# Heads in pairs, wide exponentials and a mask on GpSimd in a fused chunk-selecting attention and MLP kernel

## The chip, the cores and the metric

The kernel runs on one core of a Trainium2 chip. Its time is the device time of one launch in microseconds (us); a median over several launches is quoted with its range. A launch more than 1.5% above the fastest one of the same kernel is called slow. The profile has five rows that matter here: PE (TensorE, matrix products), PEld (its weight loads, which overlap), ACT (ScalarE), DVE (VectorE) and POOL (GpSimd). The span that a profile shows is about 2 us shorter than the device time of its launch.

A few words are used throughout. PSUM is the memory that TensorE writes its results to. Both kernels use it as eight banks, each of 512 fp32 columns on 128 partitions. A "double-bank buffer" is a tile of 1024 columns. A "buffer" comes from a pool: the program asks for the next one, and the first instruction that writes it waits until everything that used it last has finished.

## The reference, cut to what matters

```python
# q, k, v: (4, 8, 768, 64) fp32; MLP: 3072 tokens, 512 -> 2048 -> 512
k_min, k_max = min/max of k over each chunk of 32 rows        # 24 chunks per head
ub  = sum over d of max(q * k_min, q * k_max)                  # bound per query and chunk
ub  = -1e9 for chunks after the query's own
top = the 6 chunks with the largest ub, for each query
scores = q @ k.T / 8, masked to the top chunks and to j <= i
attn = softmax(scores) @ v
x = attn of all heads side by side                             # (3072, 512)
h = x @ w_in;  out = (h * clip(h + 3, 0, 6) / 6) @ w_out
```

Since max(q·a, q·b) with a ≤ b equals relu(q)·b − relu(−q)·a, the bound is one matmul of [relu(q), relu(−q)] with [k_max, −k_min]. Both kernels keep it in fp32, because it decides a ranking.

## The kernel before

It is written for one core with TensorE as the engine to fill. Attention goes head by head: `stage_A` computes the chunk selection of head n, then `stage_B` computes scores, exponentials and weighted values of head n−1. The MLP of a finished batch is cut into pieces that are dealt out between the heads of the next batch, so that TensorE has MLP work while attention waits for other engines. The order of instructions on each engine is fixed when the kernel is built: a scheduler in the build chooses it, and what it knows of the buffers enters into the choice.

```python
ps_attn = pool(bufs=4, PSUM)      # four single-bank tiles for attention
ps_mlp  = pool(bufs=4, PSUM)      # four single-bank tiles for the MLP

# stage_A, one head: k and -k side by side, fp32 transposes, max over each 32 columns
nc.vector.tensor_scalar_mul(KS[:, :, D:2 * D], KS[:, :, 0:D], -1.0)
for i in range(nb):
    nc.tensor.transpose(KT[:, i * P:(i + 1) * P], KS[:, blk, :], IDENT32[:])
nc.vector.tensor_reduce(out=KC[...], in_=KT[...], axis=X, op=max)      # k statistics
nc.scalar.copy(LHS[0:64, ...], KT[0:64, ...])
...                                                  # QPM = relu(q), relu(-q), transposed
nc.tensor.matmul(UBP[:, qb, :], lhsT=QPM[...], rhs=KC[:, :], ...)      # the bound, 6 blocks
...                                                  # top 6 -> 0/1 columns next to q in CQ

# stage_B, one head: scores up to 512 wide, causal mask as a second matmul, then exp
SPS = ps_attn.tile([P, 512])
nc.tensor.matmul(SPS[:, 0:N], lhsT=LHS[...], rhs=RHS[...], ...)
nc.tensor.matmul(SPS[:, 0:P], lhsT=IDENTB[:], rhs=TRINEG[:], ...)      # first block only
nc.scalar.activation(PTt[:, 0:N], SPS[:, 0:N], Exp, bias=NEGBIG, scale=scale)
...                                                  # PVP = PT.T @ [v, 1], one tile per block
nc.vector.reciprocal(RINV[:], PVP[:, D:D + 1])
nc.vector.tensor_scalar(Xb[:, qb, ...], PVP[:, 0:D], RINV[:, 0:1], None, op0=mult)

# one MLP hidden tile of 128 features x 384 tokens
HP = ps_mlp.tile([P, 384])
...                                                  # 4 matmuls
nc.scalar.activation(U[:], HP[:], Relu, bias=THREE)
nc.vector.scalar_tensor_tensor(out=GT[:, f, :], in0=U, scalar=6.0, in1=HP, op0=min, op1=mult)
# the second product: OP = ps_mlp.tile([P, 512]), 16 matmuls, copied out and stored
```

HP's bank is therefore held through three engines: the matmuls, then U (ScalarE reads it), then GT (VectorE reads it again).

The softmax here doesn't subtract the row's maximum and nothing guards it: scores larger than these inputs give would overflow.

## Time and profile before

| reading | before |
|---|---|
| time, median of three launches | 462.2 us (459.36 to 462.56) |
| TensorE busy | 396.5 of 459.0 us |
| share of TensorE in the chain of waits | 70% |
| first attention alone (until the first HP matmul) | 124.1 us |
| attention and MLP interleaved ("middle") | 288.0 us, 269.0 of it TensorE busy |
| MLP alone at the end ("tail") | 46.9 us |

Here are three lines of the page of the kernel before: busy time with share of the span, the granted TensorE clock in 40 slices (9 is 90% or more of full speed), and the chain of work that ended last.

```profile
PE 396.5 (86%) x3052; PEld 279.6 (61%) x3072; DVE 284.3 (62%) x1213; ACT 248.8 (54%) x537; POOL 64.1 (14%) x100
...
PEclk9999657556689999999899999998999999999999
...
PE 70%; DVE 9%; ACT 7%; DMA 7%; issue 5%; ACTq 1%; DVEq 0%
```

Next, lines from the same page's table of the costliest groups. Each gives line, engine, operation, output<-inputs, shapes and count, then busy us and the mean ns of one, then the engine's idle time before them and what ended it. They are the operations that the change replaces.

```profile
L221 ACT ACTIVATE PTt<-SPS,NEGBIG 128x512 bf16<-128x512 f32 (+3 forms) x256 | 114.9, 552 | 74.3 <-PE SPS L217 74.0
L188 PE MATMUL UBP<-KC,QPM 128*128 128x24 f32 x384 | 52.7, 279 | 21.1 <-ACT QPM L184 20.5
...
L217 PE MATMUL SPS<-TRINEG,IDENTB 128*128 128x128 bf16 x192 | 44.8, 248 | 0.0
L165 PE MATMUL KT<-IDENT_64,KS 128*128 128x128 f32 x192 | 33.0, 316 | 5.0 <-DVE KS L158 4.8
```

Matmul records overlap: the record of an HP matmul lasts 326 ns (median), while HP matmuls of one tile start 160 ns apart. So what one costs a full TensorE is the distance from one start to the next. Costs of matmuls below are such distances.

The table of stretches of the kernel before gives the three stages. Its columns are the stretch, its length, busy us and instructions of PE, PEld, DVE, ACT and POOL, then the mean granted clock, the DMA share and GB/s.

```profile
0.00:124.10 124.10, 85.03 (x549) 68.98 (x550) 70.54 (x306) 45.15 (x101) 27.73 (x56) 0.74 0.64 122
124.10:412.10 288.00, 269.02 (x2272) 187.97 (x2288) 193.92 (x866) 181.86 (x398) 36.34 (x44) 0.98 0.42 60
412.10:459.00 46.90, 42.45 (x242) 22.64 (x240) 19.86 (x43) 21.79 (x38) 0.00 (x0) 0.98 0.09 34
```

In the middle TensorE idles for only 288.0 − 269.0 = 19.0 us out of 288. VectorE and ScalarE are each busy about two thirds of the time. By every view this is a TensorE kernel: take work from TensorE and it should get faster.

### The profile page before, as it was taken

Reading aid. Unit: us, or ns where it says so; the run is one execution under the profiler, and the core shown is the slowest. Engines: PE = TensorE matmul, PEld = TensorE weight load, DVE = VectorE, ACT = ScalarE, POOL = GpSimd, SP = SyncE. Lnnn points to the kernel's source line nnn. Section 1 sums busy time; section 2 is a strip of 40 time slices with the busy share of each in tenths; the row PEclk is TensorE's granted clock in tenths of the full one; section 3 lists DMA queues with packets and bytes.
Section 4 is the critical chain, followed back from the end, with each engine's and each line's share of the span. In section 5 each row is a group of like instructions: output and inputs, shape, how many; then the busy total and the mean of one; then the engine's idle time right before and its main releaser. Section 6 shows DMA issues by size and latency. Waiting matters only on the chain.

```text
span 459.0 us, 8780 instructions
## 1 busy us (share of the span) xinstructions
PE 396.5 (86%) x3052; PEld 279.6 (61%) x3072; DVE 284.3 (62%) x1213; ACT 248.8 (54%) x537; POOL 64.1 (14%) x100
## 2 busy tenths in 40 slices
PE   2267878888889998998999999887999999999996
PEld 2255656676667666755676666555676667655552
DVE  1576675555468657865687487654786578547170
ACT  0214444434458557745686467644685577567271
POOL 8221111111101101111111111111011111000000
PEclk9999657556689999999899999998999999999999
DMA  8987854424333554355343534454435432210101
GB/s 213 240 240 152 152 87 56 53 31 52 49 44 36 94 97 53 37 91 94 40 52 50 87 67 52 52 76 93 50 36 94 81 34 19 34 47 0 70 0 69
DMA packets 107307, 34.11 MB, mean 74 GB/s; under 512 B 101120, under 2 KB 101120, under 8 KB 107264
## 3 DMA queue, kind: packets, MB, share of 16 engines
q0 software_dynamic: 50176, 6.30, 21.6%
q1 hardware_dynamic: 30272, 16.78, 13.4%
q10 hardware_dynamic: 26816, 10.49, 9.3%
q8 instruction: 24, 0.39, 0.3%
q14 instruction: 19, 0.16, 0.1%
HBM read 33.55 MB, written 6.29 MB: 87 GB/s over the span
## 4 chain that ended last, share of the span: by engine, by line
PE 70%; DVE 9%; ACT 7%; DMA 7%; issue 5%; ACTq 1%; DVEq 0%
PE OP L283 16%; PE HP L269 16%; PE SPS L214 9%; PE UBP L188 8%; PE PVP L233 7%; PE KT L165 5%; ACT PTt L221 4%; DMA KS<-in_k_dram 4%; PE CQT L199 4%; PE QT L183 3%; DMA wtmpt<-in_moe_w_in_dram 3%; PE SPS L217 2%; DVE GT L274 1%; DVE KC L166 1%; DVE UBS L191 1%
## 5 line engine op out<-in xcount | busy, mean ns | idle before, releaser
L221 ACT ACTIVATE PTt<-SPS,NEGBIG 128x512 bf16<-128x512 f32 (+3 forms) x256 | 114.9, 552 | 74.3 <-PE SPS L217 74.0
L269 PE MATMUL HP<-XT,WIN 128*128 128x384 bf16 x512 | 103.1, 328 | 6.4 <-DVE GT L274 3.9
L283 PE MATMUL OP<-WOUT,GT 128*128 128x512 bf16 x364 | 91.3, 378 | 1.9 <-DVE GT L274 1.3
L273 ACT ACTIVATE U<-HP,THREE 128x384 bf16<-128x384 f32 x128 | 70.7, 591 | 26.8 <-PE HP L269 17.6
L274 DVE SCALAR_TENSOR_TENSOR GT<-U,HP 128x384 bf16<-128x384 bf16 x128 | 67.5, 546 | 11.9 <-ACT U L273 6.8
L188 PE MATMUL UBP<-KC,QPM 128*128 128x24 f32 x384 | 52.7, 279 | 21.1 <-ACT QPM L184 20.5
L269 PEld LDWEIGHTS <-WIN 128*128 128x128 bf16 x512 | 49.4, 102 | 32.7 <-issue 11.1
L188 PEld LDWEIGHTS UBP<-KC,QPM 128*128 128x128 f32 x384 | 52.0, 208 | 28.2 <-ACT QPM L184 26.5
L154 POOL DMA_DIRECT2D CQ<-in_q_dram x32 | 29.0, 907 | 238.0 <-PE SPS L214 104.1
L283 PEld LDWEIGHTS <-GT 128*128 128x128 bf16 x384 | 35.1, 99 | 33.4 <-issue 5.9
L199 PE MATMUL CQT<-IDENTB,CQ 128*88 128x128 bf16 x192 | 36.5, 261 | 18.8 <-DVE CQ L195 18.8
L238 DVE TENSOR_SCALAR Xb<-PVP,RINV 128x64 bf16<-128x64 f32 x192 | 48.2, 279 | 2.2
L233 PE MATMUL PVP<-VB,PTt 128*128 128x65 bf16 x672 | 44.9, 205 | 4.0 <-ACT PTt L221 3.2
L237 DVE RECIPROCAL RINV<-PVP 128x1 f32<-128x1 f32 x192 | 26.9, 161 | 33.7 <-PE PVP L233 32.4
L199 PEld LDWEIGHTS <-CQ 128*88 128x88 bf16 x192 | 26.1, 141 | 34.1 <-DVE CQ L195 25.7
L233 PEld LDWEIGHTS <-PTt 128*128 128x128 bf16 x672 | 35.8, 105 | 17.8 <-issue 4.5
L166 DVE TENSOR_REDUCE KC<-KT 128x16 f32<-128x512 f32 x64 | 32.9, 549 | 19.3 <-PE QT L183 14.4
L217 PE MATMUL SPS<-TRINEG,IDENTB 128*128 128x128 bf16 x192 | 44.8, 248 | 0.0
L214 PE MATMUL SPS<-RHS,LHS_163 88*128 88x512 bf16 (+3 forms) x128 | 40.3, 353 | 0.6
L214 PE MATMUL SPS<-RHS,LHS_165 88*128 88x512 bf16 (+3 forms) x128 | 40.0, 366 | 0.5 <-ACT PTt L221 0.2
L152 POOL DMA_DIRECT2D VB<-in_v_dram x32 | 26.4, 826 | 91.8 <-DVE RINV L237 72.1
L165 PE MATMUL KT<-IDENT_64,KS 128*128 128x128 f32 x192 | 33.0, 316 | 5.0 <-DVE KS L158 4.8
(424 smaller groups left out, 397.2 us busy)
## 6 DMA issues: line engine op xcount, KB each, us to landing
KS<-in_k_dram ACTq DMA_DIRECT2D x32, 192.0 KB, 3.3
QSRC<-in_q_dram SPq DMA_DIRECT2D x32, 192.0 KB, 2.7
out_dram<-OT SPq DMA_DIRECT2D x24, 256.0 KB, 2.1
VB<-in_v_dram POOLq DMA_DIRECT2D x32, 96.0 KB, 3.3
CQ<-in_q_dram POOLq DMA_DIRECT2D x32, 96.0 KB, 3.0
wtmpt<-in_moe_w_in_dram SPq DMA_DIRECT2D x4, 512.0 KB, 7.0
wtmpt<-in_moe_w_in_dram ACTq DMA_DIRECT2D x4, 512.0 KB, 6.6
wtmpt<-in_moe_w_out_dram SPq DMA_DIRECT2D x8, 256.0 KB, 3.1
```

The lines of the kernel that those rows point to most:

```text
L165: nc.tensor.transpose(KT[:, i * P:(i + 1) * P], KS[:, blk, :], IDENT32[:])
L188: nc.tensor.matmul(UBP[:, qb, :], lhsT=QPM[:, qb * P:(qb + 1) * P], rhs=KC[:, :], start=True, stop=True)
L199: nc.tensor.transpose(CQT[:, qb * P:(qb + 1) * P], CQ[:, qb, :], IDENTB[:])
L214: nc.tensor.matmul(SPS[:, 0:N], lhsT=LHS[0:D + NCH, jb * P:(jb + 1) * P], rhs=RHS[0:D + NCH, q0:q1], start=True, stop=(not first))
L217: nc.tensor.matmul(SPS[:, 0:P], lhsT=IDENTB[:], rhs=TRINEG[:], start=False, stop=True)
L221: nc.scalar.activation(PTt[:, 0:N], SPS[:, 0:N], ACT.Exp, bias=NEGBIG[:], scale=scale)
L233: nc.tensor.matmul(PVP[:, :], lhsT=PTt[:, loc:loc + P], rhs=VB[:, jb, :], start=(jb == 0), stop=(jb == qb))
L238: nc.vector.tensor_scalar(Xb[:, qb, h * D:(h + 1) * D], PVP[:, 0:D], RINV[:, 0:1], None, op0=A.mult)
L269: nc.tensor.matmul(HP[:, :], lhsT=WIN[:, kt, f * P:(f + 1) * P], rhs=XT[:, kt, :], start=(kt == 0), stop=(kt == KT_HID - 1))
L273: nc.scalar.activation(U[:], HP[:], ACT.Relu, bias=THREE[:], scale=1.0)
L274: nc.vector.scalar_tensor_tensor(out=GT[:, f, :], in0=U[:], scalar=6.0, in1=HP[:], op0=A.min, op1=A.mult)
L283: nc.tensor.matmul(OP[:, :], lhsT=GT[:, f, t * P:(t + 1) * P], rhs=WOUT[:, f, :], start=(f == 0), stop=(f == FT - 1))
```

## The change

The intent is to take work off all three busy engines at once:

- Two heads go through `stage_A` together, so that 64-row transposes become 128-row ones; k is transposed in bf16.
- k minima and maxima are taken from a separate load of k with one chunk per partition (two reductions of 2048 elements per 128 chunks), instead of from fp32 transposes.
- The score tiles of two key blocks are packed into one tile of 896 columns, so that one exp of 896 columns replaces two or three. This needs double-bank PSUM buffers.
- HP pairs go through the same double-bank buffers, with one Relu and one product of 768 columns per pair.
- The causal mask goes from a TensorE matmul to a GpSimd select on the exp's output.
- Normalisation is one reciprocal and one product for six blocks instead of twelve operations.
- Weights are cast to bf16 by the loading DMA instead of by VectorE.

The diff, cut to its core:

```diff
-    ps_attn = pool("ps_attn", bufs=4)     # single-bank
-    ps_mlp  = pool("ps_mlp",  bufs=4)     # single-bank
+    ps_big  = pool("ps_big",  bufs=2)     # double-bank: SPS, QT and HP
+    ps_sm   = pool("ps_sm",   bufs=4)     # single-bank: all the rest
...
+        KR: 128 chunks of k, one per partition (32 rows x 64)
+        view = KR[:].rearrange("p (w d) -> p d w", d=D)
+        nc.vector.tensor_reduce(out=KM[:, 0:D], in_=view, axis=AX.X, op=A.max)
+        nc.vector.tensor_reduce(out=KM[:, D:2 * D], in_=view, axis=AX.X, op=A.min, negate=True)
...
+        QT = ps_big.tile([P, 1024], FP32, name="QT", tag="big")       # two heads of q, 5 blocks
+        QP = Relu(QT);  QN = Relu(-QT)                                # ScalarE
...
-            SPS = ps_attn.tile([P, 512]); scores; mask matmul; exp up to 512 wide
+        for ja, jb in [(0, 5), (1, 4), (2, 3)]:
+            SPS = ps_big.tile([P, 1024], FP32, name="SPS", tag="big")
...
+            nc.scalar.activation(PT[:, 0:base], SPS[:, 0:base], ACT.Exp, bias=NEGBIG[:], scale=scale)
+            nc.gpsimd.affine_select(out=dv, in_=dv, pattern=[[0, 2], [1, P]], ...)   # both diagonals
...
-                    HP = ps_mlp.tile([P, GRP]); 4 matmuls; U; GT
+                HP = ps_big.tile([P, 2, 512], FP32, name="HP", tag="big")            # two at once
+                for f in range(2):
+                    for kt in range(KT_HID):
+                        nc.tensor.matmul(HP[:, f, 0:GRP], ...)
+                nc.scalar.activation(U[:], HP[:, :, 0:GRP], ACT.Relu, bias=THREE[:], scale=1.0)
+                nc.vector.scalar_tensor_tensor(out=GT[:, f0:f0 + 2, :], in0=U[:], scalar=6.0,
+                                               in1=HP[:, :, 0:GRP], op0=A.min, op1=A.mult)
```

All eight PSUM banks are used in both kernels. What changed is their form: eight tiles in two pools became two large and four small ones, and the two large ones serve three producers.

## The prediction

> **What bounds the kernel now.** TensorE. The page shows it busy 396.5 of 459 us (86%); the chain of waits puts 70% on it; ScalarE is at 54%, VectorE at 62%. The table by stretches shows three stages:
>
> - 0-115 us: start, then attention of the first batch alone. From 46 to 115 us six heads take 11.4 us each at a granted clock of 0.57-0.64, switching between 0.50 and 1.00. That is the binary clock gate of the Trainium skill, "TensorE: Matmul & The Clock Gate", Part 1; the trace agrees.
> - 115-402 us: 24 heads with three batches' MLP, 12 us per head, clock about 0.97, TensorE about 92% busy.
> - 402-459 us: the last attention, then MLP alone: four dense bursts of about 10.2 us.
>
> **What changes, from durations in the timeline and the groups.** Start-to-start at full clock: HP matmul 160 ns, OP 215 ns, fp32 transposes 110 ns each (six in 0.66 us), UBP record 117 ns, PVP 43 ns, mask matmul (TRINEG) 56 ns, bf16 transposes about 57 ns.
>
> TensorE removed:
> - 192 mask matmuls, -11 us.
> - 384 fp32 transposes become 80 fp32 + 96 bf16 + 6: 42 to 15 us, -27 us.
> - UBP goes from 384 to 320 records, bound by weight loads, -8 us.
>
> Summed, TensorE work goes from 344 to about 300 us. MLP (165 us) and PVP (30 us) are unchanged.
>
> ScalarE: exps at 388 ns (128 wide) and 691 ns (512) give 0.79 ns per column and 0.29 us fixed; 256 exps become 96 of about 1.0 us. With paired Relus and no LHS casts, 249 to about 205 us.
>
> VectorE: loses KS/QS builds, per-block normalisation (75 us to about 23), 192 compares (45 us to 7) and weight casts (13 us); gains 12 reduces over 2048 elements. Reduces of 512 (685 ns) and 256 (413 ns) extrapolate to 2.3 us each. Their stride is 256 bytes; the Trainium skill, "SBUF — State Buffer", says each access crossing a 16-byte line pays a penalty, so perhaps 4 us; no trace shows it yet. Total 284 to about 200-220 us.
>
> GpSimd: 64 casting loads at about 0.87 us, 96 masks at about 0.4 us (from 283 ns for 128, 820 ns for 768), 16 copies: 64 to about 120 us, still not the limit.
>
> **On the critical path.** Only TensorE's saving and the start count.
> - Start: first score work at about 26 us becomes about 13.
> - Attention alone: five pairs, still mostly at half clock: about 13.2 us of TensorE work, 16.5 us per pair with gaps (before 23): about 82 us.
> - Middle: 213 us of TensorE work at 88% density (two double-bank PSUM buffers shared by scores, q transposes and MLP make it slightly looser than before): 242 us.
> - Tail: 42 us of matmul plus waits for the two HP buffers (each held about 3.4 us, so 1.7 us per HP pair against 1.28 of matmul): 48 us.
>
> Sum about 384; I say **382 us, range 350 to 415**. Faster 0.96, same 0.03, slower 0.01.
>
> **What would show it.** TensorE still leads the chain; UBP group 320 records near 40 us; mask and KT fp32 groups gone; exp group 96 of about 1.0 us; reduce 2.3 us (or about 4); attention-only stage ends near 95 us, still at clock about 0.5-0.65; tail 46-50 us.
>
> **What would make it wrong.** The half clock vanishing in the attention stage (about 350). The opposite: the two double-bank buffers, or masks queued on GpSimd behind load issues, opening TensorE gaps in the middle (density 80%: about 410). Strided reduces much slower than 4 us would delay the start and k statistics. Casting weight loads could hold up k/v loads on the same queue.

## The result, and the profile after

The median is 439.37 us (438.2 to 439.62, four runs) against 461.06 us (459.36 to 462.56, four runs) of the kernel before. The ratio is 0.951, with a 95% interval from 0.945 to 0.957. Ratios are the mean time of one kernel's fast runs over that of the other's fast runs in the same rounds, so they are not quite the ratios of the quoted medians. The change is 5% faster, where 17% was predicted, and the time lies outside the range.

The lines of the page of the kernel after that answer to those shown of before:

```profile
PE 343.7 (79%) x2598; PEld 214.9 (49%) x2614; DVE 204.1 (47%) x477; ACT 191.9 (44%) x253; POOL 117.1 (27%) x211
...
PEclk9999858999889789997999999999989999999999
...
PE 51%; DVE 18%; ACT 13%; DMA 8%; POOL 5%; issue 4%; ACTq 1%; POOLq 0%
```

Work fell on every engine that was to be relieved: TensorE by 52.8 us of busy time, VectorE by 80.2 and ScalarE by 56.9. But TensorE's share of the chain fell from 70% to 51%, while VectorE's and ScalarE's nearly doubled, although both engines are now busy less than half of the time. That pattern means waiting for one another, not a new full engine.

Four groups of the same page, the new operations:

```profile
L236 ACT ACTIVATE PT<-SPS,NEGBIG 128x896 bf16<-128x896 f32 x96 | 93.1, 1005 | 48.0 <-PE SPS L230 47.6
L285 ACT ACTIVATE U<-HP,THREE 128x768 bf16<-128x768 f32 x64 | 57.7, 901 | 84.4 <-PE HP L282 83.8
L239 POOL TENSOR_SCALAR_AFFINE_SELECT PT<-PT 128x256 bf16<-128x256 bf16 x96 | 40.3, 421 | 160.6 <-ACT PT L236 160.4
L147 DVE TENSOR_REDUCE KM<-KR 128x64 f32<-128x2048 f32 x6 | 21.8, 3632 | 2.5 <-DMA KR<-in_k_dram 2.5
```

Each agrees with what was predicted for it (about 1.0 us, none given, about 0.4 us, "perhaps 4 us"). The exp also agrees with the Trainium skill, "ScalarE: Activation LUTs", What ACT_TABLE_LOAD costs, which gives 280 ns plus 0.833 ns per column for such an instruction. By that formula an estimate for 896 columns is 1026 ns; here it took 1005 ns.

The table of stretches of the kernel after, with the same three stages (until the first HP matmul, until the last PVP matmul, the rest):

```profile
0.00:97.50 97.50, 63.06 (x518) 48.38 (x519) 69.31 (x169) 38.51 (x58) 53.29 (x92) 0.89 1.13 177
97.50:377.80 280.30, 227.55 (x1800) 139.55 (x1809) 116.75 (x287) 133.63 (x170) 63.86 (x119) 0.95 0.26 36
377.80:437.70 59.90, 53.11 (x291) 26.94 (x292) 18.07 (x22) 19.80 (x25) 0.00 (x0) 0.99 0.11 40
```

This table holds the whole result. The first stage is 26.6 us shorter and the tail, which now holds more of the MLP, is 13.0 us longer. In the middle TensorE's busy time fell by 269.0 − 227.6 = 41.5 us. The middle became only 7.7 us shorter, because TensorE's idle time rose from 19.0 to 280.3 − 227.6 = 52.8 us. The work was removed, and four fifths of the gain came back as gaps.

What the gaps waited for is in the table of waits. First the kernel before, TensorE's waits in its middle stage: who waited, for whom, then us in total, how often, the longest.

```profile
PE CQT L199 <- DVE CQ L195: 4.2, 4, 1.2
PE UBP L188 <- ACT QPM L184: 4.1, 3, 1.4
PE HP L269 <- DVE GT L274: 3.9, 5, 1.2
...
PE SPS L214 <- ACT PTt L221: 0.2, 1, 0.2
```

Then the same view of the kernel after:

```profile
PE SPS L230 <- ACT PT L236: 12.3, 13, 1.6
PE SPS L230 <- DVE GT L286: 8.7, 12, 1.1
PE PVP L248 <- POOL PT L239: 7.4, 14, 1.3
PE HP L282 <- DVE GT L286: 5.5, 8, 0.7
...
PE CQT L208 <- DVE CQ_132 L201: 3.7, 2, 2.6
...
PE QT L175 <- DVE GT L286: 2.3, 4, 0.7
PE HP L282 <- ACT PT L236: 1.0, 3, 0.7
```

Line 230 writes score tiles and line 286 is the MLP's product. A score matmul does not need any result of the MLP: where SPS waits for GT, it waits for a PSUM buffer that an HP pair held until GT had read it. Scores waiting for scores cost 0.2 us in the middle before and 12.3 us now; scores waiting for the MLP did not occur before and now take 8.7 us. All waits on the two double-bank buffers together (12.3 + 8.7 + 5.5 + 2.3 + 1.0) are 29.8 us.

How such a gap comes about can be followed in the timeline of the kernel after, across the engines. Columns are start, duration, engine, line, operation, and in brackets the engine's idle time before it with what ended that. The stretch is one head's worth, near the end of the middle.

```profile
361.80 1.46 PE L282 MATMUL HP<-XT,WIN 128*128 128x384 bf16 x8 [0.68 <-DVE GT L286]
...
363.10 0.54 PE L230 MATMUL SPS<-RHS,LHS_126 88*128 88x512 bf16 x3
363.30 0.90 ACT L285 ACTIVATE U<-HP,THREE 128x768 bf16<-128x768 f32 x1 [1.24 <-PE HP L282]
364.10 1.00 ACT L236 ACTIVATE PT<-SPS,NEGBIG 128x896 bf16<-128x896 f32 x1
364.23 0.95 DVE L286 SCALAR_TENSOR_TENSOR GT<-U,HP 128x768 bf16<-128x768 bf16 x1 [1.18 <-ACT U L285]
365.15 0.92 PE L230 MATMUL SPS<-RHS,LHS_126 88*128 88x512 bf16 x5 [1.50 <-ACT PT L236]
...
366.78 0.48 PE L282 MATMUL HP<-XT,WIN 128*128 128x384 bf16 x2 [0.66 <-ACT PT L236]
...
370.99 0.32 PE L282 MATMUL HP<-XT,WIN 128*128 128x384 bf16 x1 [0.68 <-DVE GT L286]
```

At 363.1 the first buffer holds an HP pair and the second gets the first score tile. U must read the HP pair first; the exp of the score tile comes after it on ScalarE; GT reads the HP pair meanwhile. Both buffers come free at about 365.1, and TensorE, with the next score tile due in its program order, stands still for 1.50 us. The pattern then repeats: 361.80 and 370.99 are the same point of two heads, 9.19 us apart, with 0.66 + 0.68 + 1.50 = 2.84 us of gaps between them.

A count from durations alone could have pointed to this beforehand. In this stretch a head has three HP pairs and three score tiles. An HP pair holds its buffer for at least 1.28 (eight matmuls 160 ns apart) + 0.90 (U) + 0.95 (GT) = 3.13 us. A score tile holds it for at least about 1.4 us (0.4 for its matmuls, 1.0 for the exp). Three of each are 13.6 us, 6.8 us for each of two buffers, before any hand-off between engines is counted. TensorE has 9.19 − 2.84 = 6.35 us of work there. So in such a head the buffers, not TensorE, are the tighter limit. This is an estimate from the durations shown, and it holds for such heads only: the program deals out three pieces of MLP per head, and of the 24 pieces of a batch 16 are HP pairs, so four of eight heads have three pairs, two have two and two have none.

The Trainium skill, "Perfetto Trace Analysis", Optimization Strategy, describes just this sign: a gap that keeps repeating on the engine that should be saturated can mean too little PSUM for the next tile. The trace agrees: gaps of 0.68 and 1.50 us come again 9.19 us later.

### The profile page after: what moved, and what is told of

Read it like the earlier page. It is cut to its first block, busy times and chain, and to the rows that moved or that the text cites. A ratio compares the mean times of both kernels' runs of the same rounds, so it can differ in the third digit from the quotient of the medians.

```text
span 437.7 us, 6521 instructions
## 1 busy us (share of the span) xinstructions
PE 343.7 (79%) x2598; PEld 214.9 (49%) x2614; DVE 204.1 (47%) x477; ACT 191.9 (44%) x253; POOL 117.1 (27%) x211
## 4 chain that ended last, share of the span: by engine, by line
PE 51%; DVE 18%; ACT 13%; DMA 8%; POOL 5%; issue 4%; ACTq 1%; POOLq 0%
PE OP L295 16%; PE HP L282 13%; ACT PT L236 5%; PE PVP L248 5%; ACT U L285 5%; DVE GT L286 4%; DMA VB<-in_v_dram 4%; PE SPS L230 3%; PE UBP L194 3%; DVE KM L147 3%; DVE KM L148 3%; PE CQT L208 3%; PE UBP L193 3%; DMA QS<-in_q_dram 3%; POOL PT L239 2%
## 5 line engine op out<-in xcount | busy, mean ns | idle before, releaser
L236 ACT ACTIVATE PT<-SPS,NEGBIG 128x896 bf16<-128x896 f32 x96 | 93.1, 1005 | 48.0 <-PE SPS L230 47.6
L285 ACT ACTIVATE U<-HP,THREE 128x768 bf16<-128x768 f32 x64 | 57.7, 901 | 84.4 <-PE HP L282 83.8
L286 DVE SCALAR_TENSOR_TENSOR GT<-U,HP 128x768 bf16<-128x768 bf16 x64 | 61.0, 952 | 48.5 <-ACT U L285 48.4
L239 POOL TENSOR_SCALAR_AFFINE_SELECT PT<-PT 128x256 bf16<-128x256 bf16 x96 | 40.3, 421 | 160.6 <-ACT PT L236 160.4
L248 PE MATMUL PVP<-VB,PT 128*128 128x65 bf16 x672 | 40.7, 206 | 16.9 <-POOL PT L239 16.1
L248 PEld LDWEIGHTS <-PT 128*128 128x128 bf16 x672 | 32.5, 105 | 42.1 <-POOL PT L239 36.2
L193 PE MATMUL UBP<-KCBP,QP 128*128 128x48 f32 x160 | 34.2, 298 | 6.3 <-ACT QP L178 4.6
L194 PE MATMUL UBP<-KCBN,QN 128*128 128x48 f32 x160 | 34.1, 298 | 0.9 <-ACT QN L180 0.5
L193 PEld LDWEIGHTS UBP<-KCBP,QP 128*128 128x128 f32 x160 | 27.0, 212 | 9.5 <-ACT QP L178 7.5
L85 POOL DMA_DIRECT2D VB<-in_v_dram x32 | 26.6, 837 | 10.8 <-PE PVP L248 9.6
L194 PEld LDWEIGHTS UBP<-KCBN,QN 128*128 128x128 f32 x160 | 27.1, 213 | 2.4 <-ACT QN L180 2.1
L147 DVE TENSOR_REDUCE KM<-KR 128x64 f32<-128x2048 f32 x6 | 21.8, 3632 | 2.5 <-DMA KR<-in_k_dram 2.5
```

The source lines that it names most:

```text
L147: nc.vector.tensor_reduce(out=KM[:, 0:D], in_=view, axis=AX.X, op=A.max)
L193: nc.tensor.matmul(o, lhsT=QP[:, i * P:(i + 1) * P], rhs=KCBP[:, kc], start=True, stop=False)
L194: nc.tensor.matmul(o, lhsT=QN[:, i * P:(i + 1) * P], rhs=KCBN[:, kc], start=False, stop=True)
L236: nc.scalar.activation(PT[:, 0:base], SPS[:, 0:base], ACT.Exp, bias=NEGBIG[:], scale=scale)
L239: nc.gpsimd.affine_select(out=dv, in_=dv, pattern=[[0, 2], [1, P]], compare_op=A.is_ge, fill=0.0, base=0, channel_multiplier=-1)
L248: nc.tensor.matmul(PVP[:, qb, :], lhsT=PT[:, loc:loc + P], rhs=VB[:, e, j, :], start=(j == 0), stop=(j == qb))
```

## The experiments

These are the theories, with the letters that the expectations use. Theory A: the two double-bank buffers, shared by scores, q transposes and HP pairs, opened the gaps. A2, a variant: the fused pair as such (768-wide Relu and product) is too long, whatever buffer it is in. Theory B: GpSimd is the cause, by its masks and by what its queue waits for. Theory C: the slow strided k reductions on VectorE delay everything that needs VectorE. Theory D came later: weight loads crowd the first stage. All variants are edits of the kernel after and gave correct results unless said otherwise. In this summary "ratio" is to the kernel before in the same rounds.

| variant | median us (range) | ratio | first / middle / tail us |
|---|---|---|---|
| before | 461.06 (459.36 to 462.56) | 1 | 124.1 / 288.0 / 46.9 |
| after | 439.37 (438.2 to 439.62) | 0.951 | 97.5 / 280.3 / 59.9 |
| e1_hp_single | 391.84 (389.74 to 393.97) | 0.848 | 101.3 / 234.0 / 56.6 |
| e2_mask_pe | 439.96 (436.56 to 444.81) | 0.950 | 99.7 / 280.8 / 60.2 |
| e3_kstat_free (wrong) | 435.89 (433.56 to 438.76) | 0.944 | 98.0 / 273.6 / 59.9 |
| e4_vb_const | 432.12 (430.45 to 433.62) | 0.934 | 92.4 / 279.3 / 59.8 |
| e5_big3 | 432.13 (424.92 to 432.23) | none | 113.4 / 259.8 / 56.9 (slow) |
| e6_hp_single_in_big | 451.59 (450.57 to 455.84) | 0.979 | 98.6 / 295.2 / 60.3 |
| e7_unpacked | 400.01 (397.07 to 403.93) | 0.864 | 99.6 / 246.7 / 55.7 (slow) |
| e8_hp_defer | 390.49 (389.69 to 391.24) | 0.845 | 95.9 / 235.1 / 56.6 |
| e9_hp_vb_defer | 384.56 (380.21 to 388.17) | 0.834 | 88.9 / 236.0 / 56.6 |
| e10_all | 380.1 (377.89 to 381.76) | 0.826 | 92.7 / 228.0 / 56.6 |
| e11_hp_mask_pe | 394.79 (394.31 to 395.98) | 0.858 | 101.8 / 233.8 / 57.0 |
| e12_hp_kfree (wrong) | 394.81 (393.67 to 397.09) | 0.858 | 98.5 / 236.5 / 56.6 |
| e13_two_small | 469.69 (464.04 to 472.03) | 1.010 | 113.5 / 296.2 / 60.3 (slow) |
| e18_three_again (e5_big3 again) | 434.79 (431.75 to 436.28) | 0.942 | 112.0 / 263.8 / 56.9 |
| e14_three_order_of_two | 443.12 (440.81 to 446.39) | 0.961 | 110.0 / 271.5 / 57.2 |
| e17_two_order_of_three | 469.76 (464.49 to 472.78) | 1.015 | 114.7 / 285.4 / 62.7 |
| e16_after_order_of_three | 460.39 (457.85 to 463.07) | 0.998 | 111.4 / 282.1 / 62.3 |

"(slow)" marks a profile that fell on a run called slow; such a profile is not compared with others here. One caution holds for the whole table: every edit makes the build choose a somewhat different order on every engine, so a variant shows its edit together with the order that goes with it. How much an order can be worth is measured further down (e14, e16, e17).

### HP out of the double-bank buffers (e1_hp_single)

```diff
-                HP = ps_big.tile([P, 2, 512], FP32, name="HP", tag="big")     # pair, U and GT 768 wide
+                for f in range(f0, f0 + 2):
+                    HP = ps_sm.tile([P, GRP], FP32, name="HP", tag="ps")      # single, U and GT 384 wide
```

> The changed kernel with one thing undone: the MLP's first product (HP) goes one 384-wide tile at a time into the four single-bank PSUM buffers, so the two double-bank buffers serve only scores and q transposes; U and GT become 128 instructions of 384 again. Theory A (TensorE waits in the middle stage because scores, q transposes and HP share two double-bank buffers; 29.8 us of its 51 us of waits there name them): TensorE waits of scores on GT and of HP on GT go, the middle stage (289 us, from the first HP to the last attention) falls by 20 to 30 us, total 410 to 420. Theories B (masks on GpSimd) and C (k reductions on VectorE): within 4 us of 439, or some us slower for the 64 more ScalarE and VectorE instructions.

It took 391.84 us, 47.5 less than the kernel after, which is more than expected. The table of stretches of e1_hp_single:

```profile
0.00:101.30 101.30, 62.58 (x534) 48.30 (x535) 70.55 (x170) 38.59 (x58) 53.76 (x93) 0.88 1.10 170
101.30:335.30 234.00, 214.13 (x1786) 134.21 (x1794) 120.70 (x334) 142.05 (x218) 63.16 (x119) 0.99 0.31 43
335.30:391.90 56.60, 52.09 (x292) 27.18 (x291) 20.26 (x38) 23.57 (x41) 0.00 (x0) 1.00 0.11 42
```

The gain is in the middle: 46.3 of the 47.5 us. ScalarE and VectorE have more work there than in the kernel after (142.1 against 133.6 us, 120.7 against 116.8), because the narrow operations pay their fixed part twice, and yet the stage is a sixth shorter. The largest of TensorE's waits in the middle of e1_hp_single:

```profile
PE SPS L230 <- ACT PT L236: 8.3, 10, 1.1
PE CQT L208 <- DVE CQ L201: 2.5, 3, 1.3
PE QT L175 <- ACT PT L236: 2.3, 1, 2.3
PE PVP L248 <- POOL PT L239: 2.0, 8, 0.4
```

SPS no longer waits for GT at all. Of the 46.3 us, TensorE's idle time gives 52.8 − (234.0 − 214.1) = 32.9 us. The other 13.4 us are TensorE's busy time, 227.6 against 214.1 us for the same matmuls. The granted clock fits that: 0.95 in the middle of the kernel after is, with a clock of either half or full speed, some 28 us at half speed (0.05 × 280 × 2), and 0.99 is some 5 us; read in steps of 3 us, it is 27 and 7 us. Half of the difference is lost, 10 to 12 us. This is an estimate. That the gaps cause the half clock is not shown. They vanish together here, but from 358 to 376 us, where the gaps of the timeline above lie, the clock stayed full, and e18_three_again below has 20 us fewer gaps than e17_two_order_of_three at a clock of 0.91 against 0.92. The Trainium skill, "TensorE: Matmul & The Clock Gate", A second HAM failure mode: psum-queue depth-cycling, describes a case of this kind: short idling between groups of matmuls, as PSUM buffers cycle, makes the clock swing between half and full.

The waits on the mask (7.4 to 2.0 us) and on VectorE's selection (7.3 to 2.5 us, both CQT lines of after together) fell as well, though nothing was done to masks or selection. So most of these waits, too, went when the sharing ended.

### The mask back on TensorE (e2_mask_pe)

```diff
-            nc.gpsimd.affine_select(out=dv, in_=dv, ...)
+                    if c == 0:
+                        nc.tensor.matmul(SPS[:, base:base + P], lhsT=IDENTB[:], rhs=TRINEG[:],
+                                         start=False, stop=True)
```

> The changed kernel with the causal mask back on TensorE (192 small matmuls of about 56 ns, 11 us in all), no masks on GpSimd. Theory B (the mask on GpSimd stands between exp and PVP, 0.42 us each plus whatever its queue holds in front): the 16 us of PVP waits on GpSimd go and the total falls by 8 to 20 us, to 419 to 431. Theory A and C: TensorE has 11 us more to do and the waits for buffers stay, total 439 to 450.

It took 439.96 us, the same as after. The waits for GpSimd's mask (7.4 us in the middle) are gone, about 11 us of matmuls (192 of 56 ns) came onto TensorE, and the middle stayed at 280.8 us. The edit removes a wait and adds work, and the two can cancel: in the middle TensorE's busy time rose from 227.6 to 236.9 us and its idle time fell from 52.8 to 43.9 us. So the run does not show that masks or TensorE's work are free. It does show that the mask on GpSimd costs no more than the matmuls that it replaced; as the cause of a miss of some 57 us, the masks' part of theory B falls.

### k reductions almost free (e3_kstat_free, wrong on purpose)

```diff
-        view = KR[:].rearrange("p (w d) -> p d w", d=D)
+        view = KR[:, 0:2 * D].rearrange("p (w d) -> p d w", d=D)      # 2 of 32 rows
```

> The changed kernel with the twelve k reductions over 2 of each chunk's 32 rows instead of 32 (wrong results on purpose): about 40 us of VectorE go, everything else stays. Theory C (reductions of 3.6 us, two in a row in front of the selection chain, stall TensorE and let its clock drop to half): total 409 to 424, no drop of the clock near 150 us. Theories A and B: at most 8 us faster, 431 to 440, mostly from the start.

It took 435.89 us, 3.5 less. The result is wrong (relative error 0.60), since only two rows of each chunk are seen; the rest of the program is unchanged, though the build chose another order for TensorE, VectorE, ScalarE and GpSimd. VectorE lost about 37 us of work and the kernel hardly noticed. Theory C falls as an explanation of a miss of some 57 us.

### v in fixed tiles (e4_vb_const)

```diff
-        VB = src.tile([P, 2, NBLK, D + 1], BF16, name="VB", tag="vb")
+        VB = VB_tiles[(b * NPAIR + hp) % 3]           # the column of ones written once, at the start
...
-        nc.gpsimd.memset(VB[:, :, :, D:D + 1], 1.0)
```

> The changed kernel with v in three fixed tiles whose ones column is written once at the start on VectorE, so that no memset on GpSimd waits for the v load to land (57 us of such waits) with masks and load issues behind it in the queue. Theory B: the hole of 6.3 us at 56 to 62 us goes and the start of the pair loop tightens, total 427 to 434. Theories A and C: the hole moves to another wait, total 435 to 440.

It took 432.12 us, 7.2 less. This part of theory B holds: the timeline of GpSimd in the kernel after shows what was taken away.

```profile
50.87 0.76 POOL L141 DMA_DIRECT2D WOUT<-in_moe_w_out_dram  x1
62.07 0.15 POOL L86 MEMSET VB<- 128x12 bf16 x1 [10.44 <-DMA VB<-in_v_dram]
62.13 0.76 POOL L239 TENSOR_SCALAR_AFFINE_SELECT PT<-PT 128x256 bf16<-128x256 bf16 x2
```

The write of the column of ones goes to the tile that a DMA is filling, so GpSimd's queue stood for 10.44 us until the load had landed, and the masks stood behind it. TensorE waited up to 6.3 us for those. With fixed tiles the first stage took 92.4 us instead of 97.5.

### Single HP tiles, still from the double-bank buffers (e6_hp_single_in_big)

```diff
-                    HP = ps_sm.tile([P, GRP], FP32, name="HP", tag="ps")      # e1
+                    HP = ps_big.tile([P, GRP], FP32, name="HP", tag="big")
```

> The changed kernel with HP in single 384-wide tiles, U and GT unfused, as in the run of 392 us, but the tiles still taken from the two double-bank buffers. A (few buffers, shared): no gain, 437 to 460, for a tile of half the work holds a buffer for more than half the time. A2 (the fused pair's hold time, or the fusing as such): most of the gain of the run of 392 us, 395 to 415.

It took 451.59 us, 12 more than after and 60 more than e1_hp_single, from which it differs in one pool name. The largest of TensorE's waits in its middle:

```profile
PE HP L282 <- DVE GT L286: 15.3, 27, 1.0
PE SPS L230 <- DVE GT L286: 9.8, 18, 0.9
```

The narrow operations are the same ones as in e1_hp_single. So the width of U and GT, A2, is not the cause; which buffers HP takes is. (60 us is also far more than an order was seen to cost below.) With single tiles each double-bank buffer carries half as much work for each turn, and the waits for GT grow from 8.7 + 5.5 to 25.1 us. The Trainium skill, "Perfetto Trace Analysis", Optimizing Scalar/DVE Operations, says that breaking up instructions may help when ScalarE or VectorE are not saturated but cause gaps elsewhere. Here that alone cost 12 us; it came with a gain only together with other buffers.

### A third double-bank buffer, and its control (e5_big3, e13_two_small, e18_three_again)

```diff
-    ps_big = pool("ps_big", bufs=2)   # after
-    ps_sm  = pool("ps_sm",  bufs=4)
+    ps_big = pool("ps_big", bufs=3)   # e5_big3 and e18_three_again; 2 in e13_two_small
+    ps_sm  = pool("ps_sm",  bufs=2)   # all three
```

> The changed kernel with three double-bank PSUM buffers and two single-bank ones, instead of two and four; nothing else. If the cause is that scores, q transposes and HP share too few double-bank buffers (A), the waits of scores and HP on GT shrink and the total falls well below 439, to 400 to 425, less than the 392 of the run with HP on its own because the small buffers now are two. If it is the fused pair itself, the long hold of 2 banks by one ScalarE and one VectorE instruction (A2), a third buffer hides it too; if it is neither, 432 to 450.

> The changed kernel with two small single-bank PSUM buffers instead of four, two double-bank ones as it has; two of eight banks lie idle. It is the control of the run with three double-bank and two small ones (432 us, middle stage 259.8 us). If the third double-bank buffer is what shortened the middle stage, this one takes 275 to 300 us there and 450 to 475 in all. If the third double-bank buffer does nothing and the rearranged program did it, within 8 us of 432.

> e5_big3 unchanged, on the same chip as the three runs with fixed orders, because it had only one fast run: 422 to 434 us by both theories.

A third double-bank buffer has to be paid for with two of the small ones, so e5_big3 alone mixes a gain and a loss. It had one fast run of 424.92 us and three called slow at 432.1 to 432.2, so it has no ratio; repeated as e18_three_again on another chip it took 434.79 us, with four fast runs and a ratio of 0.942. That is outside of the 400 to 425 us that theory A had led to expect, and in the range that stood for neither theory. The control e13_two_small shows why, for it pays the price without the purchase: 469.69 us, ratio 1.010, as expected of it. The third buffer is thus worth about 35 us between the medians, or 32 us by the ratios, which leave out slow launches and compare within the same rounds. The control also shows the other side: 30 us between 439.37 and 469.69 us (27 by the ratios) for two small buffers fewer.

### Buffers or order? (e14_three_order_of_two, e17_two_order_of_three, e16_after_order_of_three)

A comparison of the two builds showed that e5_big3 and e13_two_small differ in more than a count: the scheduler had put TensorE's instructions into another order. So the 35 us might come from the order alone. To separate the two, the order of one build was written into the other, on TensorE, VectorE, ScalarE and GpSimd, by edges that fix the sequence and add no wait:

```diff
+    for name, runs in ORDER.items():              # the order of the other build, engine by engine
+        seq = [per[name][i] for first, n in runs for i in range(first, first + n)]
+        for a, c in zip(seq, seq[1:]):
+            tc.add_manual_dep(c, a.name, ..., reason="order")
```

The builds were compared again afterwards: the sequences of these engines were then the same, instruction by instruction, and so are the sequences of TensorE and VectorE records in the traces.

> The build reorders each engine's instructions, and another count of buffers gives another order. This run has the buffers of e5_big3 (3 double-bank, 2 small) with every engine's order fixed to that of e13_two_small (2 double-bank, 2 small). Theory R (the buffers themselves, at run time): the time stays near e5_big3, 424 to 438 us. Theory O (the order that the build makes of the buffers): it goes to e13_two_small, 460 to 472. Both halves: 440 to 458.

> The buffers of e13_two_small (2 double-bank, 2 small) in the order of e5_big3. Theory R: 462 us or more (an order made for other buffers may be worse still). Theory O: 424 to 438 us, as e5_big3.

> The kernel after (2 double-bank, 4 small) in the order of e5_big3. Theory R: 432 to 448 us, as the kernel after, since its waits on the double-bank buffers stay. Theory O: below 425, since it has the order of e5_big3 and two small buffers more.

| | order made for two | order made for three |
|---|---|---|
| two double-bank buffers, two small | 469.69 us (1.010) | 469.76 us (1.015) |
| three double-bank buffers, two small | 443.12 us (0.961) | 434.79 us (0.942) |

With the order held, the third buffer gives 26.6 us in one column and 35.0 in the other. (Both medians with two double-bank buffers include a launch called slow, and e13_two_small ran on another chip; by the ratios it is 23 and 34 us.) With the buffers held, the order made for three gives nothing in one row and 8.3 us in the other. So most of the gain is the buffer itself, as it comes free at run time, and the rest is that the build can use it; 443.12 us stands at the lower edge of what was expected for "both halves". The middle stages of the two kernels that have the same instructions in the same order show it; first e17_two_order_of_three:

```profile
114.70:400.10 285.40, 235.72 (x1781) 145.99 (x1790) 115.77 (x283) 134.49 (x170) 62.93 (x118) 0.92 0.26 35
```

And e18_three_again, whose order it has:

```profile
112.00:375.80 263.80, 234.36 (x1783) 145.79 (x1792) 115.06 (x283) 131.10 (x170) 63.37 (x118) 0.91 0.28 38
```

TensorE is busy for 235.7 and 234.4 us. The stage is 21.6 us shorter, and all but 1.4 us of that is idle time that is gone. The waits say which: a score tile's wait for GT, whose result it does not use, in e17_two_order_of_three and then in e18_three_again, in the middle of each.

```profile
PE SPS L230 <- DVE GT L286: 21.5, 31, 1.1
...
PE SPS L230 <- DVE GT L286: 6.4, 14, 0.7
```

Theory A therefore stands, by two independent tests: moving one producer out (e1_hp_single against e6_hp_single_in_big) and adding one buffer with all else held.

e16_after_order_of_three was a miss for both theories: the kernel after in the order of e5_big3 took 460.39 us, 21 more than in its own order. (In that one order, and in the same rounds, the three double-bank buffers of e18_three_again are 26 us faster than its two, in spite of two small buffers fewer.) An order made for other buffers can thus cost 21 us. This bounds what the small differences may be read for: 3 us or 7 us between two variants can be their edit or the order that the build made of it.

The part of the order in the 47.5 us of e1_hp_single is open.

### No packing at all (e7_unpacked)

```diff
-    ps_big (2 double-bank) + ps_sm (4)
+    ps_mlp (4 single-bank: HP, XTP, OP) + ps_sm (4 single-bank: attention)
-    one exp of 896 per two key blocks; QT in one tile of 1024
+    one exp of up to 512 per score tile; QT in two tiles of 512; one mask for each diagonal block
```

> The changed kernel with the PSUM plan of before: all eight buffers single-bank, four for attention and four for MLP; exps of up to 512 columns (256 of them instead of 96), QT in two tiles, one mask per diagonal block; batched normalisation, pairs, k statistics, bf16 k transposes and casting loads stay. If the double-bank packing is worth its buffers once HP is apart, this is slower than 392 us: 395 to 410, ScalarE busy about 240 us. If the double-bank tiles are what costs, 380 to 392.

It took 400.01 us, as expected, with ScalarE busy for 226.6 us (about 240 expected), against 204.2 in e1_hp_single (that profile of e7 fell on a slow run). The pools of the kernel before, under the new arithmetic, are thus worth nearly 40 us over the kernel after. The packing of the exps itself, e7_unpacked against e1_hp_single, is worth about 8 us between the medians, once HP is out of its way; the intervals of the two ratios, 0.842 to 0.855 and 0.854 to 0.874, still touch, so this is not clear of noise.

### What bounds e1_hp_single next (e11_hp_mask_pe, e12_hp_kfree, e8_hp_defer)

Each is e1_hp_single with one more edit: the mask matmul of e2, the shortened reductions of e3 (wrong), and weight loads begun at one for each pair instead of two:

```diff
-        if idx < NPAIR:
-            for _ in range(2): weight_dmas.pop(0)()
+        for _ in range(1 if idx < NPAIR else 2): weight_dmas.pop(0)()      # if any are left
```

> HP in single tiles from the small buffers, and the mask back on TensorE. In the changed kernel 11 us more of TensorE work cost nothing (439.96 against 439.37 us). If that was because its middle stage waits for buffers and not for TensorE, the same 11 us count here, where those waits are gone: 398 to 404 against 392. If the mask on GpSimd costs as much as it saves in any case: 390 to 394.

> HP in single tiles from the small buffers, k reductions over 2 of 32 rows (wrong on purpose): 40 us of VectorE less. If the reductions hold the chain only where VectorE is otherwise free (as in the changed kernel, 3.5 us): 386 to 390. If they are the next limit once the buffers are apart: 370 to 380.

> The run of 392 us (HP single, from the small buffers) with the weight loads later: one per pair for four pairs, then two, instead of two per pair for four pairs. Theory D (the attention-only stage, 101 us there, waits for loads: 16 DMA engines are busy over 90% to 66 us and q, k and v stand behind weights and k rows): that stage falls to 84 to 94 us, total 376 to 386. Rival (it is bound by TensorE at half clock, as the prediction had it): within 4 us of 392.

The first came out between its two expectations, the second outside of both, and the third as its rival said. With the mask on TensorE the time rose by 3 us only (4.5 by the ratios), to 394.79, where the 11 us of matmuls should have counted nearly in full if e1_hp_single were bound by TensorE's work. The middle did not become longer at all (233.8 us); part of that is the clock, which read 1.00 there and 0.99, with 7 us at half speed, in the middle of e1_hp_single. The remaining gaps, 10.6 us for double-bank buffers, can take in some of it, so e1_hp_single is near that bound and not at it. Free k reductions gave nothing (394.81 us), so VectorE's reductions do not look like the next limit either. Deferred weight loads shortened the first stage of the profile by 5.4 us, but the time only by 1.4 (390.49 us), so theory D falls as it was stated; the rival, "within 4 us of 392", fits, though its reason, half clock, was not tested by this. Each of these kernels has an order of its own, and none of these differences is beyond what that can do.

### Combinations (e9_hp_vb_defer, e10_all)

e9_hp_vb_defer has the edits of e1, e4 and e8. e10_all adds two more: the second block of k is loaded on ScalarE's queue, behind the first q loads, and the two strided reductions become a tree of contiguous maxima and minima:

```diff
-        nc.vector.tensor_reduce(out=KM[:, 0:D], in_=view, axis=AX.X, op=A.max)
-        nc.vector.tensor_reduce(out=KM[:, D:2 * D], in_=view, axis=AX.X, op=A.min, negate=True)
+        nc.vector.tensor_tensor(out=TM[:, 0, :], in0=KR[:, 0:HALF], in1=KR[:, HALF:2 * HALF], op=A.max)
+        nc.vector.tensor_tensor(out=TM[:, 1, :], in0=KR[:, 0:HALF], in1=KR[:, HALF:2 * HALF], op=A.min)
+        ...                                           # halved again until 64 columns are left
```

> HP in single tiles from the small buffers, v in fixed tiles with the ones column written once, and the weights deferred: the three edits that were each not slower, together. If their effects add (47, 7 and 1 us): 380 to 386. If the v edit only bought slack that HP's own buffers already give: 388 to 393.

> The same three edits, and the start reordered: the second block of k rows is loaded on the ScalarE queue behind the first q loads, which waited 11.4 us for a share of the DMA engines; and the k statistics as a tree of contiguous maxima and minima (12 to 14 VectorE instructions per block[...], in place of two strided reduces of 3.6 us). If the first stage waits for these: 370 to 380. If it is bound by TensorE at half clock: within 3 us of the run without these two.

They took 384.56 and 380.1 us. The first is what adding the three effects gives (380 to 386). The second lies between its two expectations, and the first stage, which the reordered start was to shorten, became longer (88.9 to 92.7 us). e10_all is correct and beats both kernels: its ratio to before is 0.826 (0.822 to 0.829). The tree takes about 6.5 us of VectorE time for each block of 128 chunks, against 7.2 us for two strided reductions, so little of the gain is its saving in work. The gain is in the middle, which fell from 236.0 to 228.0 us, and nearly all of that is TensorE busy time (218.0 to 210.5 us) at a clock of 0.99 instead of 0.96. Whether it comes of eleven short instructions in place of two long ones is not shown: no run separates the two edits from each other and from the order, so that stays open.

## Why the prediction was wrong

**What was right.** The costs of single operations were right. Exps measured 1005 ns (about 1.0 predicted), masks 421 ns (0.4), casting loads 839 and 837 ns (0.87), the reduce 3632 ns ("perhaps 4"). Busy times were right: ScalarE 191.9 us (205), VectorE 204.1 (200 to 220), GpSimd 117.1 (120). The UBP records were spaced by 111 ns, so 320 of them are 35.6 us (about 40). The first stage ended at 97.5 us (95). TensorE still leads the chain, with 51%.

**The step that failed** is this one: "Middle: 213 us of TensorE work at 88% density (two double-bank PSUM buffers shared by scores, q transposes and MLP make it slightly looser than before): 242 us." The prediction ends its middle at the last OP matmul of the third batch, somewhat later than the tables above. By its own boundaries:

| stage | predicted | after | e1_hp_single |
|---|---|---|---|
| start and attention alone | 95 | 97.5 | 101.3 |
| middle | 242 | 289.0 | 242.9 |
| tail | 48 | 51.2 | 47.7 |

The density was 213/289 = 74%, not 88%. With HP out of the double-bank buffers it was 213/242.9 = 88%, and the predicted 242 us came out to within 1 us. That closeness is in part luck: TensorE was measured busy for 223.0 of the 242.9 us there, a density of 92% and 10 us more work than predicted, and the two errors cancel (in the kernel after it was busy for 236.2 of the 289.0 us, in part at half clock). So the work was counted to about 5% and the density was assumed. The mechanism was named, but its size was put down as "slightly looser" without being worked out. Even the case listed as the failure, "density 80%: about 410", was too mild. The miss of the middle, 47 us, is nearly the whole miss of 57 us.

The sum that was missing stands in the prediction itself, one line further down. For the tail it reckons that each buffer is held for about 3.4 us, so a pair can go every 1.7 us though its matmuls take 1.28. The tail came out 3 us over. The same reckoning was not made for the middle, where the score tiles come in as well; done there, it gives at least 6.8 us for a head of three pairs against 6.35 us of TensorE work, before hand-offs. It would have said that the buffers bind in these heads, but not how much: 0.45 us in each of 12 such heads is some 5 of the 47 us. What the rest is made of, hand-offs between engines, waiting in program order or half clock, is not divided by any run.

The other dangers that the prediction listed were real but small: masks behind load issues on GpSimd's queue, 7 us in all (e4_vb_const); the reductions, 3.5 us (e3_kstat_free); the mask itself, nothing beyond the 11 us of matmuls that it replaced (e2_mask_pe). With the order free in each, these are sizes within some us.

**The first stage** was right in number, partly for other reasons. The prediction expected half clock throughout; the page of after shows mostly full clock (0.89 as a mean), and in its place waits: 14.0 us for the first loads of q, 8.7 us on masks. But the clock of the page is not to be trusted at the start. Two stretches of the timeline of the kernel after show the same instructions early and late:

```profile
19.52 0.63 PE L194 MATMUL UBP<-KCBN,QN 128*128 128x48 f32 x2
19.95 0.63 PE L193 MATMUL UBP<-KCBP,QP 128*128 128x48 f32 x2
...
143.24 0.39 PE L193 MATMUL UBP<-KCBP,QP 128*128 128x48 f32 x2
143.46 0.39 PE L194 MATMUL UBP<-KCBN,QN 128*128 128x48 f32 x2
```

Starts are 0.43 us apart at 19.5 us and 0.22 us apart at 143 us, so the early ones ran at half the rate, in a stretch where the page's clock reads full. That half the rate is half the clock shows at about 51.5 us of the same profile: there the page's clock falls to 0.50, and pairs of these records go from 0.22 to 0.43 us apart. The prediction's half clock was thus real for at least a part of this stage.

**What stays open.** How the 46.3 us that e1_hp_single gains in the middle divide into waits removed and clock regained is an estimate, and how much of them is the order that its build could choose is not known; with the third buffer that part was 8 of 35 us between the medians. What makes the clock fall in the middle is open too. Why the mask matmuls cost e1_hp_single so little, and what bounds the first stage (88.9 to 101.8 us with four small buffers and the order that the build made for them, 111.4 us in the order of three), was not settled.

## What to carry to other kernels

Before merging small tiles into large ones, list for each PSUM buffer who writes it, how long each tile holds it through all its readers, and divide the sum by the number of buffers; if the result comes near the busy engine's own time, the removed work may come back as gaps. A wait for an engine whose result the waiting instruction does not use is a wait for a buffer, and a table of waits in which it is new is worth more than the busy shares. Test it by moving one producer to another pool and by adding one buffer with a control that pays the same price, since a shorter instruction in the same pool (451.6 us here) can point the wrong way; and hold the order of instructions while doing so, if the build chooses it.

## What the Trainium skill lacked or had wrong

- "TensorE: Matmul & The Clock Gate", Part 1, says that the clock falls to half after an idle window of about 3.4 us. In the middle of the kernel after no wait of TensorE was longer than 2.6 us, and the mean clock still fell to 0.95 (0.99 in e1_hp_single). It fell to half at about 147 us, before that longest wait, after 3 us with TensorE busy for 2.4. The page's own later section on psum-queue cycling, which needs short idling only, agrees with this better, but does not say when it happens: with 2.84 us of gaps in 9.19 (361.80 to 370.99 us) the clock stayed full.
- The same page warns that clock events in traces are unreliable. A number for it from here: the clock read full at 19.5 us while UBP records came 0.43 us apart for two, against 0.22 us at 143 us. Here the events are missing rather than wrong: the packed trace holds no clock record before about 48 us.
- "SBUF — State Buffer", Specifications (TRN2), names a penalty for crossing 16-byte lines but gives no size. Here a reduce over 2048 fp32 elements with a stride of 256 bytes took 3632 ns, 1.77 ns an element, while contiguous reduces of the kernel before (685 ns for 512 and 413 ns for 256) give 1.06 ns for each further element. Those read PSUM and not SBUF, so the stride's own part is not isolated.
- No page gives a duration for GpSimd's affine select: 421 ns here for two diagonal blocks of 128 columns in bf16.
- No page puts a figure on PSUM buffers shared by several producers. Here one double-bank buffer more was worth 23 to 34 us of 470 in two orders held fixed, two single-bank buffers fewer cost 27 to 30 us with the order free, and taking one producer out of a shared pair of buffers gave 47.5 us of 439.
- "Perfetto Trace Analysis", Optimizing Scalar/DVE Operations, says that breaking up instructions that cause gaps elsewhere may help when ScalarE and VectorE are not saturated (44% and 47% busy here), and does not name the buffers as a condition. In the same buffers it made the kernel 12 us slower (451.59 against 439.37 us); with other buffers it came with the gain of 47.5 us.
